# P.V in the step of its own scores, exp in four masked pieces, and a reordered last projection in a cached-attention decode kernel

## The chip, the cores and the metric

The kernel runs on one core of a Trainium2 chip. Times are device microseconds (us) of one launch. A profiled execution also gives a trace; its span (first to last instruction) is some 2 us under the launch time. Engines are PE (matrix products; PEld is its weight load), DVE (vector), ACT (activation functions), POOL, and SP, whose queue issues nearly all loads. "Rate" is what the DMA engines moved, in GB/s. The granted clock is the share of PE's full clock that the trace shows as granted.

All comparisons use runs in the fast state; a run counts as slow when it is over 1.5% above the fastest of its kernel. A ratio is the mean time of one kernel's fast runs over that of the other's fast runs of the same rounds, so it is not quite the ratio of the medians that are quoted.

## The reference

One decode step for four sequences, in bf16: attention over a cache, then an MLP, each behind a layernorm, with residuals.

```python
q = layernorm(x) @ wq                        # x [4,1,640], wq [640, 32*128]
scores = einsum("bhqd,bhkd->bhqk", q, k_cache) * 128 ** -0.5   # k_cache [4,32,4096,128]
o = einsum("bhqk,bhkd->bhqd", softmax(scores), v_cache)        # v_cache as k_cache
h = x + o.reshape(4, 1, 4096) @ wo           # wo [4096, 640]
hm = layernorm(h) @ w1 + b1                  # w1 [640, 1728]
out = h + (hm * tanh(softplus(hm))) @ w2     # w2 [1728, 640]
```

The two caches are 134 MB each; they are nearly all of the 283 MB that the kernel reads, and each byte is used once.

## The kernel before

The work is cut into 32 tiles, one for each group of four heads and each sequence. A tile is 4 MB of K and 4 MB of V. Partition p holds 128 keys of head p // 32. All K and V tiles go through a pool of four slots of 32 KB per partition; a load waits until a slot is free.

```python
NSLOT = 4; G = 4; PG = 32; R = 128; RS = 32; NSUB = 4; NE = 3
...
loads = []                                  # order: k0 v0 k1 v1 ... k29 v29 k30 k31 v30 v31 wo w1 w2
...
def issue_loads(upto):                      # called as issue_loads(i + 1) at the start of step i
    while loads and not (upto < NT and upto in kt and upto in vt):
        f, *a = loads.pop(0)
        f(*a)
```

A tile is handled in four parts s. DVE multiplies K by q, PE folds the products of 128 columns to 16 by adding them in PSUM (the memory that takes its sums), DVE sums these to scores. After the fourth part ACT takes exp four times, once for each head: head g sits in 32 partitions, and its exp is written to column g of a buffer that was cleared once, so that P.V gets a block-diagonal left side.

```python
def emit_scores(i, s):
    ...
    nc.vector.tensor_reduce(out=s_t[i][:, s * RS : (s + 1) * RS], in_=reds.pop((i, s))[:, :, :], ...)
    if s == NSUB - 1:
        for g in range(G):
            sl = slice(g * PG, (g + 1) * PG)
            nc.scalar.activation(out=e_bufs[i % NE][sl, :, g], in_=s_t[i][sl, :], func=ACT.Exp,
                scale=SCALE, accum_out=rs_bufs[hg % 2][sl, b, g : g + 1])
...
for i in range(NT):
    issue_loads(i + LA)
    for s in range(NSUB):
        emit_mult(i, s)
        if s > 0:
            emit_scores(i, s - 1)
        elif i > 0:
            emit_scores(i - 1, NSUB - 1)     # last part of the tile before
            ...
        emit_fold(i, s)
        if i > 0 and i < last:
            emit_pv(i - 1, s)                # P.V of the tile before
        ...
```

After the loop come P.V of the last tiles and the last projection. For each group k, `emit_wo(k)` permutes the attention output on PE, copies it to bf16 on DVE and multiplies it by `wo`.

```python
emit_pv(last, 2); emit_pv(last, 3); emit_pv_copy(last)
for k in range(WLATE, NWB - 1):             # groups 4, 5, 6
    emit_wo(k)
emit_o(last); emit_ot(NHG - 1); emit_wo(NWB - 1)
```

The softmax here doesn't subtract the row's maximum and nothing guards it: scores larger than these inputs give would overflow.

## Time and profile before

| | before |
|---|---|
| time, median of the first 3 runs | 686.46 us (682.96 to 686.54) |
| span of the profiled run | 682.5 us |
| busy: PE, DVE, ACT | 65%, 56%, 14% |
| moved over DMA | 283.8 MB |

The page of the profile, its share line and its DMA lines. In the DMA line each digit is the busy share of one fortieth of the span, in tenths; the next line has the GB/s of the same slices.

```profile
PE 444.8 (65%) x2933; PEld 179.6 (26%) x2933; DVE 380.9 (56%) x329; ACT 96.2 (14%) x311; POOL 3.6 (1%) x14
...
DMA  9999999999999999999999999999999999999991
GB/s 366 438 427 432 418 438 431 429 404 436 429 427 419 431 432 429 434 425 416 442 428 436 414 432 433 427 421 427 432 434 422 414 430 430 430 397 425 415 412 69
```

No engine but the DMA is near its limit. The DMA is busy to the end of the 39th slice. The rate is not flat. Between the second slice and the 39th it goes from 397 to 442 while the busy digit stays at 9.

Now one step of the loop, from the timeline (start, duration, engine and line, what it does; in brackets the idle time before and what ended it):

```profile
206.22 2.29 DVE L284 TENSOR_TENSOR prod<-k_1049,qbc 128x4096 bf16<-128x4096 bf16 x1 [3.04 <-DMA k_1049<-in_A_k_cache_dram]
...
219.56 2.28 DVE L284 TENSOR_TENSOR prod<-k_1049,qbc 128x4096 bf16<-128x4096 bf16 x1
...
221.87 0.33 SPq L95 DMA_DIRECT2D v_1150<-in_A_v_cache_dram  x1
...
225.25 0.33 SPq L95 DMA_DIRECT2D k_1304<-in_A_k_cache_dram  x1
...
226.30 2.29 DVE L284 TENSOR_TENSOR prod<-k_1148,qbc 128x4096 bf16<-128x4096 bf16 x1 [3.27 <-DMA k_1148<-in_A_k_cache_dram]
```

The tile `k_1049` is worked from 206.2. The V of the next tile, `v_1150`, is issued only when the last multiply of this one ends (221.84), because the other three slots are still held: by the V of the tile before (its P.V runs in this step), by this tile's V and by the next K. At that moment the only other load under way is `k_1148`, which lands 4.4 us later; by issues less bytes moved, 1.0 MB was left to move.

The stretch from 10 to 640 us, from the view by windows (busy time of PE, PEld, DVE, ACT and POOL, then granted PE clock, DMA share, GB/s):

```profile
10.00:640.00 630.00, 413.21 (x2513) 158.58 (x2513) 361.18 (x268) 86.77 (x289) 0.00 (x0) 0.82 1.00 427
```

And the tail on PE, with one copy on DVE, from the timeline:

```profile
652.27 0.60 PE L320 MATMUL l_ps<-rs_136,ones_f 128*128 128x16 f32 x2 [2.90 <-ACT e_130 L313]
...
652.81 3.59 PE L332 MATMUL pv_122<-v_3298,e_128 128*16 128x512 bf16 x32
...
656.18 1.92 PE L332 MATMUL pv_124<-v_3392,e_130 128*16 128x512 bf16 x16
...
659.33 1.04 PE L332 MATMUL pv_124<-v_3392,e_130 128*16 128x512 bf16 x16
...
664.32 1.85 PE L353 MATMUL o_ps<-selo,pv_sb 128*128 128x4 f32 x8
...
668.00 0.18 DVE L440 COPY st<-y_ps 128x20 f32<-128x20 f32 x1 [0.77 <-PE y_ps L385]
...
670.80 4.72 PE L497 MATMUL h_ps<-ln_3821,w_slot 128*64 128x4 bf16 x70 [1.60 <-DVE ln_3821 L477]
```

PE waits 2.9 us for the last tile's exp, then does P.V of the last two tiles, then the projections one after another; from the last P.V group to the copy of the projection's sum (`y_ps`) it is 8.7 us. The MLP's first product starts at 670.8.

### The profile page before, as it was taken

To read this page: it belongs to the slowest core of one execution; us is meant where nothing else is said; L and a number is where in the kernel's file an instruction comes from. 1 tells how busy PE (TensorE), PEld (TensorE's weight loads), DVE (VectorE), ACT (ScalarE), POOL (GpSimd) and SP (SyncE) were. 2 spreads that over 40 slices of the span, in tenths; PEclk is the share of its full clock that TensorE was granted. 3 is DMA by queue.
4 is the path that set the end of the run, shared out by engine and by line. 5 is a ranking of instruction groups with operands and counts; after the bars stand their busy time and mean duration, and the time that the engine had idled before them with its cause. 6 is when DMAs were issued, how large, how long until landed. Compare 5 with 4: busy or idle time off the path is not lost.

```text
span 682.5 us, 6833 instructions
## 1 busy us (share of the span) xinstructions
PE 444.8 (65%) x2933; PEld 179.6 (26%) x2933; DVE 380.9 (56%) x329; ACT 96.2 (14%) x311; POOL 3.6 (1%) x14
## 2 busy tenths in 40 slices
PE   1836674773676844786647756767547777475876
PEld 0312221231223312232212322223112222121445
DVE  3445565583566744756645755666546556547902
ACT  0301111110111111011111101111111011111121
POOL 2000000000000000000000000000000000000000
PEclk9968976887877867989768888688788887678975
DMA  9999999999999999999999999999999999999991
GB/s 366 438 427 432 418 438 431 429 404 436 429 427 419 431 432 429 434 425 416 442 428 436 414 432 433 427 421 427 432 434 422 414 430 430 430 397 425 415 412 69
DMA packets 13014, 283.80 MB, mean 416 GB/s; under 512 B 1652, under 2 KB 1720, under 8 KB 3768
## 3 DMA queue, kind: packets, MB, share of 16 engines
q1 hardware_dynamic: 12656, 283.27, 97.4%
q8 instruction: 23, 0.38, 0.2%
q10 hardware_dynamic: 328, 0.09, 0.1%
q14 instruction: 7, 0.06, 0.0%
HBM read 283.35 MB, written 0.01 MB: 415 GB/s over the span
## 4 chain that ended last, share of the span: by engine, by line
DMA 53%; PE 33%; DVE 8%; ACT 3%; issue 2%; DVEq 0%; ACTq 0%
PE red L296 20%; DVE prod L284 6%; PE pv_124 L332 5%; DMA k_1846<-in_A_k_cache_dram 4%; DMA k_1400<-in_A_k_cache_dram 4%; DMA k_3100<-in_A_k_cache_dram 4%; DMA k_412<-in_A_k_cache_dram 4%; DMA k_2290<-in_A_k_cache_dram 4%; DMA k_2695<-in_A_k_cache_dram 4%; DMA k_603<-in_A_k_cache_dram 3%; DMA k_2040<-in_A_k_cache_dram 3%; DMA k_3294<-in_A_k_cache_dram 3%; DMA k_858<-in_A_k_cache_dram 3%; DMA k_2484<-in_A_k_cache_dram 3%; DMA k_1594<-in_A_k_cache_dram 3%; DMA k_1148<-in_A_k_cache_dram 3%
## 5 line engine op out<-in xcount | busy, mean ns | idle before, releaser
L296 PE MATMUL red<-prod,ident 128*128 128x512 bf16 x1024 | 297.2, 443 | 142.1 <-DVE prod L284 141.8
L296 PEld LDWEIGHTS <-ident 128*128 128x128 bf16 x1024 | 107.2, 111 | 310.2 <-issue 242.3
L305 DVE TENSOR_REDUCE s_f<-red 128x32 f32<-128x512 f32 x128 | 87.9, 687 | 34.3 <-PE red L296 33.9
L353 PEld LDWEIGHTS o_ps<-selo,pv_sb 128*128 128x128 f32 x256 | 32.2, 197 | 13.5 <-issue 10.3
L343 ACT COPY pv_sb<-pv_122 128x512 f32<-128x512 f32 x16 | 9.4, 586 | 183.0 <-PE pv_122 L332 183.0
L353 PE MATMUL o_ps<-selo,pv_sb 128*128 128x4 f32 x256 | 34.8, 259 | 0.0
L343 ACT COPY pv_sb<-pv_124 128x512 f32<-128x512 f32 x16 | 9.4, 586 | 171.4 <-PE pv_124 L332 171.4
L313 ACT ACTIVATE e_130<-s_f 32x128 bf16<-32x128 f32 x44 | 21.3, 485 | 61.4 <-DVE s_f L305 60.8
L313 ACT ACTIVATE e_128<-s_f 32x128 bf16<-32x128 f32 x44 | 21.3, 484 | 52.8 <-DVE s_f L305 52.3
L313 ACT ACTIVATE e_132<-s_f 32x128 bf16<-32x128 f32 x40 | 19.4, 484 | 54.0 <-DVE s_f L305 53.6
L320 PE MATMUL l_ps<-rs_134,ones_f 128*128 128x16 f32 x8 | 2.4, 381 | 37.6 <-ACT e_128 L313 19.2
L320 PE MATMUL l_ps<-rs_136,ones_f 128*128 128x16 f32 x8 | 2.4, 381 | 31.6 <-ACT e_132 L313 9.7
L284 DVE TENSOR_TENSOR prod<-k_82,qbc 128x4096 bf16<-128x4096 bf16 x4 | 9.1, 2284 | 17.7 <-DMA k_82<-in_A_k_cache_dram 17.7
L359 DVE TENSOR_TENSOR OT<-o_ps,rl 128x16 bf16<-128x16 f32 x8 | 1.6, 195 | 28.1 <-PE o_ps L353 28.1
L284 DVE TENSOR_TENSOR prod<-k_858,qbc 128x4096 bf16<-128x4096 bf16 x4 | 9.1, 2284 | 10.3 <-DMA k_858<-in_A_k_cache_dram 10.3
L284 DVE TENSOR_TENSOR prod<-k_1750,qbc 128x4096 bf16<-128x4096 bf16 x4 | 9.1, 2284 | 9.7 <-DMA k_1750<-in_A_k_cache_dram 9.7
L284 DVE TENSOR_TENSOR prod<-k_248,qbc 128x4096 bf16<-128x4096 bf16 x4 | 9.1, 2284 | 9.4 <-DMA k_248<-in_A_k_cache_dram 9.4
L284 DVE TENSOR_TENSOR prod<-k_412,qbc 128x4096 bf16<-128x4096 bf16 x4 | 9.1, 2285 | 9.4 <-DMA k_412<-in_A_k_cache_dram 9.4
L284 DVE TENSOR_TENSOR prod<-k_1304,qbc 128x4096 bf16<-128x4096 bf16 x4 | 9.1, 2284 | 9.3 <-DMA k_1304<-in_A_k_cache_dram 9.3
L326 DVE RECIPROCAL rl<-l_ps 128x16 f32<-128x16 f32 x8 | 2.1, 258 | 21.9 <-PE l_ps L320 21.9
L256 PE MATMUL q_ps<-wq_74,lnT 128*4 128x512 bf16 x32 | 11.1, 470 | 3.9 <-DMA wq_74<-in_A_wq_dram 3.9
L284 DVE TENSOR_TENSOR prod<-k_2194,qbc 128x4096 bf16<-128x4096 bf16 x4 | 9.1, 2284 | 8.0 <-DMA k_2194<-in_A_k_cache_dram 8.0
(159 smaller groups left out, 460.4 us busy)
## 6 DMA issues: line engine op xcount, KB each, us to landing
wq_74<-in_A_wq_dram SPq DMA_DIRECT2D x4, 1024.0 KB, 9.7
k_82<-in_A_k_cache_dram SPq DMA_DIRECT2D x1, 4096.0 KB, 20.5
v_84<-in_A_v_cache_dram SPq DMA_DIRECT2D x1, 4096.0 KB
k_248<-in_A_k_cache_dram SPq DMA_DIRECT2D x1, 4096.0 KB
v_250<-in_A_v_cache_dram SPq DMA_DIRECT2D x1, 4096.0 KB
k_300<-in_A_k_cache_dram SPq DMA_DIRECT2D x1, 4096.0 KB
v_302<-in_A_v_cache_dram SPq DMA_DIRECT2D x1, 4096.0 KB, 16.8
k_412<-in_A_k_cache_dram SPq DMA_DIRECT2D x1, 4096.0 KB
```

The source lines that it names most:

```text
L256: nc.tensor.matmul(q_ps[:, :], lhsT=lnT[:, c, :], rhs=wq_t[c // WQC][:, o : o + 512], start=(c == 0), stop=(c == DC - 1),)
L284: nc.vector.tensor_tensor(out=t[:, :, :], in0=kt[i][:, s * RS : (s + 1) * RS, :], in1=q_bc[hg][:, b, :].unsqueeze(1).to_broadcast([P, RS, ...
L296: nc.tensor.matmul(red[:, :, :], lhsT=ident[:, :], rhs=t[:, :, c * CW : (c + 1) * CW], start=(c == 0), stop=(c == Dh // CW - 1),)
L305: nc.vector.tensor_reduce(out=s_t[i][:, s * RS : (s + 1) * RS], in_=reds.pop((i, s))[:, :, :], axis=AX.X, op=ALU.add,)
L313: nc.scalar.activation(out=e_bufs[i % NE][sl, :, g], in_=s_t[i][sl, :], func=ACT.Exp, scale=SCALE, accum_out=rs_bufs[hg % 2][sl, b, g : g ...
L320: nc.tensor.matmul(l_ps[hg][:, :], lhsT=ones_f[:, :], rhs=rs_bufs[hg % 2][:, :, :].rearrange("p b g -> p (b g)"), start=True, stop=True,)
L326: nc.vector.reciprocal(out=rl[hg][:, :], in_=l_ps.pop(hg)[:, :])
L332: nc.tensor.matmul(pvs[i % 2][k * QD : k * QD + RQ * G, :], lhsT=e_bufs[i % NE][:, u * RQ : (u + 1) * RQ, :], rhs=vt[i][:, u * RQ : (u + 1 ...
L343: nc.scalar.copy(out=pv_sb[i][:, :, :].rearrange("p r d -> p (r d)"), in_=pvs[i % 2][:, :])
L353: nc.tensor.matmul(o_ps[hg][:, b, :], lhsT=t[:, r, :], rhs=selo[:, r, :], start=(r == 0), stop=(r == RQ - 1),)
L359: nc.vector.tensor_tensor(out=OT[:, hg * G : (hg + 1) * G, :].rearrange("p g b -> p b g"), in0=o_ps.pop(hg)[:, :, :], in1=rl.pop(hg)[:, :] ...
```

## The change

It aims at freeing V slots a step earlier, at a shorter chain after the last scores, and at a shorter tail. P.V of tile i moves from step i+1 to the end of step i. Exp is taken after each quarter of a tile on all 128 partitions, and a 0/1 mask on DVE spreads it over the four head columns. In the tail, permutations of earlier groups are done in their own steps, and the weight products are ordered to fill waits. The list of loads is rewritten but gives the same order.

```diff
+        nc.scalar.activation(                      # emit_scores, every s
+            out=ex_t[i][:, sl], in_=s_t[i][:, sl], func=ACT.Exp,
+            scale=SCALE, accum_out=rs_t[hg][:, b, s : s + 1],
+        )
+    def emit_mask(i, s):
+        nc.vector.tensor_tensor(
+            out=e_t[i][:, sl, :],
+            in0=ex_t[i][:, sl].unsqueeze(2).to_broadcast([P, RS, G]),
+            in1=hmask[:, :].unsqueeze(1).to_broadcast([P, RS, G]), op=ALU.mult)
 ... (the three cleared e buffers and two rs buffers go; the sums are masked too)
             if s > 0:
                 emit_scores(i, s - 1)
-            elif i > 0:
-                emit_scores(i - 1, NSUB - 1)
-            ...
+            if s > 1:
+                emit_mask(i, s - 2)
             emit_fold(i, s)
-            if i > 0 and i < last:
-                emit_pv(i - 1, s)
+            ... emit_o(i - 1), emit_ot, emit_perm, emit_wo of the group before at s = 1, 2, 3
+        emit_scores(i, NSUB - 1)
+        emit_mask(i, NSUB - 2)
+        emit_mask(i, NSUB - 1)
+        if i < last - 1:
+            for s in range(NSUB):
+                emit_pv(i, s)
+            emit_pv_copy(i)
 ... (tail)
-    for k in range(WLATE, NWB - 1):
-        emit_wo(k)
     emit_o(last)
     emit_ot(NHG - 1)
-    emit_wo(NWB - 1)
+    emit_wo(WLATE)
+    emit_wo(WLATE + 1)
+    emit_perm(NHG - 1)
+    emit_wo(WLATE + 2)
+    emit_wo(WLATE + 3)
 ... (layernorm: the square moves from DVE to ACT, 1/D into the matrix of ones)
```

More of the change, by code (lines that the diff above doesn't have):

```diff
@@ L137 @@
         loads.append((load_cache, kt, A_k_cache, i, "k"))
-        if i < NT - 2:
-            loads.append((load_cache, vt, A_v_cache, i, "v"))
-    loads.append((load_cache, kt, A_k_cache, NT - 1, "k"))
-    loads.append((load_cache, vt, A_v_cache, NT - 2, "v"))
+        if i == NT - 2:
+            loads.append((load_cache, kt, A_k_cache, NT - 1, "k"))
+        loads.append((load_cache, vt, A_v_cache, i, "v"))
     loads.append((load_cache, vt, A_v_cache, NT - 1, "v", 4))
@@ L196 @@
     )
-    for k in range(NE):
-        e = consts.tile([P, R, G], BF16, name=f"e{k}")
-        nc.gpsimd.memset(e[:, :, :], 0.0)
-        e_bufs.append(e)
-    rs_bufs = []
-    for k in range(2):
-        r = consts.tile([P, N, G], FP32, name=f"rs{k}")
-        nc.gpsimd.memset(r[:, :, :], 0.0)
-        rs_bufs.append(r)
+    hmask_f = consts.tile([P, G], FP32)
+    hmask = consts.tile([P, G], BF16)
+    nc.vector.tensor_reduce(
+        out=hmask_f[:, :], in_=ident[:, :].rearrange("p (g q) -> p g q", g=G), axis=AX.X, op=ALU.add
+    )
+    nc.vector.tensor_copy(out=hmask[:, :], in_=hmask_f[:, :])
+    ones_d = consts.tile([P, P], FP32)
+    nc.vector.memset(ones_d[:, :], 1.0 / D)
     IW = D // CG
@@ L300, in emit_fold @@
         reds[i, s] = red
+    e_t, ex_t, rs_t = {}, {}, {}
     def emit_scores(i, s):
+        hg, b = tiles[i]
         if s == 0:
             s_t[i] = work.tile([P, R], FP32, tag="s_f", name="s_f")
+            ex_t[i] = work.tile([P, R], BF16, tag="ex", name="ex")
+            e_t[i] = work.tile([P, R, G], BF16, tag="e", name="e", bufs=NE)
+            if b == 0:
+                rs_t[hg] = work.tile([P, N, NSUB], FP32, tag="rs", name="rs")
+        sl = slice(s * RS, (s + 1) * RS)
         nc.vector.tensor_reduce(
-            out=s_t[i][:, s * RS : (s + 1) * RS], in_=reds.pop((i, s))[:, :, :],
-            axis=AX.X, op=ALU.add,
-        )
-        if s == NSUB - 1:
-            hg, b = tiles[i]
-            for g in range(G):
-                sl = slice(g * PG, (g + 1) * PG)
-                nc.scalar.activation(
-                    out=e_bufs[i % NE][sl, :, g], in_=s_t[i][sl, :], func=ACT.Exp,
-                    scale=SCALE, accum_out=rs_bufs[hg % 2][sl, b, g : g + 1],
-                )
-    def emit_sum(hg):
+            out=s_t[i][:, sl], in_=reds.pop((i, s))[:, :, :], axis=AX.X, op=ALU.add
+        )
+        nc.scalar.activation(
+            out=ex_t[i][:, sl], in_=s_t[i][:, sl], func=ACT.Exp,
+            scale=SCALE, accum_out=rs_t[hg][:, b, s : s + 1],
+        )
+    def emit_mask(i, s):
+        sl = slice(s * RS, (s + 1) * RS)
+        nc.vector.tensor_tensor(
+            out=e_t[i][:, sl, :],
+            in0=ex_t[i][:, sl].unsqueeze(2).to_broadcast([P, RS, G]),
+            in1=hmask[:, :].unsqueeze(1).to_broadcast([P, RS, G]),
+            op=ALU.mult,
+        )
+    def emit_sum(hg):
+        rs1 = work.tile([P, N], FP32, tag="rs1", name="rs1")
+        nc.vector.tensor_reduce(
+            out=rs1[:, :], in_=rs_t.pop(hg)[:, :, :], axis=AX.X, op=ALU.add
+        )
+        rsm = work.tile([P, N, G], FP32, tag="rsm", name="rsm")
+        nc.vector.tensor_tensor(
+            out=rsm[:, :, :], in0=rs1[:, :].unsqueeze(2).to_broadcast([P, N, G]),
+            in1=hmask[:, :].unsqueeze(1).to_broadcast([P, N, G]), op=ALU.mult,
+        )
         l_ps[hg] = ps.tile([P, N * G], FP32, tag="misc", name="l_ps")
@@ L321, in emit_sum @@
             l_ps[hg][:, :], lhsT=ones_f[:, :],
-            rhs=rs_bufs[hg % 2][:, :, :].rearrange("p b g -> p (b g)"),
-            start=True, stop=True,
+            rhs=rsm[:, :, :].rearrange("p b g -> p (b g)"), start=True, stop=True,
         )
@@ L333, in emit_pv @@
                 pvs[i % 2][k * QD : k * QD + RQ * G, :],
-                lhsT=e_bufs[i % NE][:, u * RQ : (u + 1) * RQ, :],
+                lhsT=e_t[i][:, u * RQ : (u + 1) * RQ, :],
                 rhs=vt[i][:, u * RQ : (u + 1) * RQ, :],
@@ L369, with emit_perm @@
     )
-    def emit_wo(k):
+    a_t = {}
+    def emit_perm(k):
         a_ps = ps.tile([P, WB, N], FP32, tag="misc", name="a_ps")
@@ L379, in emit_wo @@
                 )
-        a = work.tile([P, WB, N], BF16, tag="a", name="a_bf")
-        nc.vector.tensor_copy(out=a[:, :, :], in_=a_ps[:, :, :])
+        a_t[k] = consts.tile([P, WB, N], BF16, name=f"a{k}")
+        nc.vector.tensor_copy(out=a_t[k][:, :, :], in_=a_ps[:, :, :])
+    def emit_wo(k):
         t = wo_t.pop(k)
@@ L385, in emit_wo @@
                 nc.tensor.matmul(
-                    y_ps[:, c, :], lhsT=t[:, j, c * P : (c + 1) * P], rhs=a[:, j, :],
+                    y_ps[:, c, :], lhsT=t[:, j, c * P : (c + 1) * P], rhs=a_t[k][:, j, :],
                     start=False, stop=(k == NWB - 1 and j == WB - 1 and c == DC - 1),
@@ L403 @@
                 emit_scores(i, s - 1)
-            elif i > 0:
-                emit_scores(i - 1, NSUB - 1)
-                if b == 0:
-                    emit_sum(hg - 1)
-            emit_fold(i, s)
-            if i > 0 and i < last:
-                emit_pv(i - 1, s)
-            if i > 1 and s == 1:
-                emit_o(i - 2)
-                if b == 1:
-                    emit_ot(hg - 1)
-                    if hg <= WLATE:
-                        emit_wo(hg - 1)
-        if i == last:
-            emit_scores(i, NSUB - 1)
+            if s > 1:
+                emit_mask(i, s - 2)
+            emit_fold(i, s)
+            if i > 0 and s == 1 and i < last:
+                emit_o(i - 1)
+                if b == 0:
+                    emit_ot(hg - 1)
+            if b == 0 and i > 0 and s == 2:
+                emit_perm(hg - 1)
+            if b == 0 and i > 0 and s == 3 and hg <= WLATE:
+                emit_wo(hg - 1)
+        emit_scores(i, NSUB - 1)
[5 more added lines that the diff above has]
+            emit_pv_copy(i)
+        if b == N - 1:
             emit_sum(hg)
-            for s in range(NSUB):
-                emit_pv(i - 1, s)
-        if i > 0:
-            emit_pv_copy(i - 1)
         if b == 1 and hg + 1 < NHG:
             emit_qbc(hg + 1)
+    for s in range(NSUB):
+        emit_pv(last - 1, s)
+    emit_pv_copy(last - 1)
     emit_pv(last, 0)
@@ L431 @@
     emit_pv_copy(last)
-    for k in range(WLATE, NWB - 1):
-        emit_wo(k)
     emit_o(last)
     emit_ot(NHG - 1)
-    emit_wo(NWB - 1)
+    emit_wo(WLATE)
[3 more added lines that the diff above has]
+    emit_wo(WLATE + 3)
     st = consts.tile([P, 2, DC, N], FP32)
     nc.vector.tensor_copy(out=st[:, 0, :, :], in_=y_ps[:, :, :])
-    nc.vector.tensor_tensor(
-        out=st[:, 1, :, :], in0=st[:, 0, :, :], in1=st[:, 0, :, :], op=ALU.mult
-    )
+    nc.scalar.activation(out=st[:, 1, :, :], in_=y_ps[:, :, :], func=ACT.Square)
     s_ps = ps.tile([P, 2 * DC * N], FP32, tag="misc", name="s_ps")
     nc.tensor.matmul(
-        s_ps[:, :], lhsT=ones_f[:, :], rhs=st[:, :, :, :].rearrange("p k c n -> p (k c n)"),
+        s_ps[:, :], lhsT=ones_d[:, :], rhs=st[:, :, :, :].rearrange("p k c n -> p (k c n)"),
         start=True, stop=True,
@@ L460 @@
     )
-    nc.vector.tensor_scalar_mul(out=mu[:, :, :], in0=mu[:, :, :], scalar1=1.0 / D)
     msq = consts.tile([P, N], FP32)
```

## The prediction

> **What bounds it now.** The load stream. The page's slice table has the DMA engines at nine tenths or more in 39 of 40 slices; in one-microsecond windows all but a last fraction of the 283.8 MB has moved by 668 us of 682.5 (about 426 GB/s from 3 us on). The Trainium skill (DMA: Bandwidth & Descriptors, Specifications) gives a fabric ceiling of 435 GB/s, so about 2% of rate is left; the best stretches here hold 431 to 438. PE is busy 65%, DVE 56%, ACT 14%. In the timeline DVE waits 2.5 to 10 us for each K tile. A serial tail follows: y_ps complete at 667.97, layernorm to 670.8, first MLP product 4.7, mish 1.7, second product 2.2, store: 14.5 us without loads.
>
> **What the change does.**
> 1. Loads. Their order is unchanged; slots come free earlier. Before, P.V of tile i-1 runs in step i, so three slots are held when loads of tile i+1 are wanted: in the timeline its v is issued only after the last multiply of tile i (221.9 us; its K lands at 226.3), the K after that when P.V ends (225.3). Bytes issued but not moved fall under 1 MB in many steps. After, both slots of tile i-1 are free at the end of step i-1, so k and v of i+1 go out one tile (4.2 MB, about 9.8 us) earlier; I estimate that 7 MB stay outstanding. In ten- and twenty-microsecond windows the trace moves 418 to 422 GB/s where outstanding bytes fell below 1 MB, 431 where they did not (overall 427). All at 431, the stream ends 6 us earlier; I count on 4.
> 2. Tail. Permutations of groups 4 to 6 (each 0.55, a 0.17 cast, 0.6 of waits) leave the tail; wo(4), wo(5) fill the wait for OT, wo(6) that for the last cast. From the last P.V product (660.3) to y_ps I count 5.2 us for 7.7: 2.5 saved. Square on ACT beside the copy, and 1/D folded into the ones matrix, save 0.3. I expect no further ACT table load.
> 3. Cost. Four masks per tile on DVE, estimated 0.25 us each from the small DVE operations here; exp in four 128x32 pieces is no dearer than four 32x128 ones of 0.485+0.25. P.V waits for its last mask, and DVE has no multiply ahead of the last reduction: about 3 us bubble per step. I estimate a step of 17 to 18 us against 19.5 of loads, so it hides. At the end it costs perhaps 1 us.
>
> **Sum.** About 4 + 2.8 - 1 = 6 us, 0.9%. Predicted 680.3 us, range 674 to 686. Chance of faster by over 2%: 0.09; within 2%: 0.87; slower by over 2%: 0.04.
>
> **What would show each step.** (1) V issues no longer follow the multiplies of the tile before by a few us; the DMA rate over 10 to 640 us rises from 427 to 430 or more; DVE still waits several us for K. (2) From last P.V product to the y_ps copy about 5 us; one group of perm matmuls there. (3) Mask operations near 0.25 us; every step ends before the next K lands.
>
> **What would make it wrong.** If rate dips are the memory's own, only the tail's 2 us remain. If a step at the slow PE clock (0.5 granted in stretches) exceeds 19.5 us, the kernel becomes compute bound and slower. If the stream ends earlier but the last tile's chain does not follow, less is gained.

## The result

| | before | after |
|---|---|---|
| median, first comparison (4 runs each) | 685.25 us (682.96 to 686.54) | 675.52 us (674.76 to 677.62) |
| ratio of fast runs | | 0.9867 (95%: 0.9828 to 0.9905) |
| two more comparisons, medians of fast runs (11 runs before each) | 683.29, 684.00 | 677.03, 676.90; ratios 0.9912, 0.9896 |
| span of the profiled run | 682.5 | 673.0 |

So the change wins 0.9% to 1.3%, 6 to 9 us. The same lines after, first the page:

```profile
PE 431.2 (64%) x2933; PEld 192.9 (29%) x2933; DVE 410.7 (61%) x474; ACT 75.4 (11%) x312; POOL 1.9 (0%) x9
...
DMA  9999999999999999999999999999999999999993
GB/s 368 425 428 434 442 427 422 432 434 439 428 424 432 433 437 428 425 429 435 433 430 428 429 429 435 428 432 433 432 429 430 431 429 433 430 430 433 414 415 160
```

DVE has become busier and the kernel faster: DVE did not bound it. The rate line is flatter; between the second and the 37th slice nothing is under 422. The windows:

```profile
10.00:640.00 630.00, 406.91 (x2574) 176.68 (x2574) 392.95 (x410) 68.10 (x295) 0.00 (x0) 0.84 1.00 431
```

427 has become 431. One step of the loop, from the timeline:

```profile
203.85 0.33 SPq L95 DMA_DIRECT2D k_1292<-in_A_k_cache_dram  x1
...
208.77 4.49 DVE L283 TENSOR_TENSOR prod<-k_1150,qbc 128x4096 bf16<-128x4096 bf16 x2
...
209.80 0.33 SPq L95 DMA_DIRECT2D v_1294<-in_A_v_cache_dram  x1
...
224.96 2.29 DVE L283 TENSOR_TENSOR prod<-k_1292,qbc 128x4096 bf16<-128x4096 bf16 x1 [2.55 <-DMA k_1292<-in_A_k_cache_dram]
```

K and V of a tile now both go out at the end of the step two before their own, K after the last multiply and V after P.V: `k_1292` at 203.85 and `v_1294` at 209.80, and `k_1292` is waited for until 224.96, 21 us after its issue. That time is not what changed: before, `k_1148` went out at 205.40 and was waited for until 226.30, 21 us as well. What changed is how much was still to be moved at the moments when a slot came free: 1.0 MB when `v_1150` went out before, 3.7 MB when `k_1292` goes out after. The tail:

```profile
649.35 0.39 PE L340 MATMUL l_ps<-rsm,ones_f 128*128 128x16 f32 x2 [1.75 <-DVE rsm L335]
...
649.68 1.90 PE L351 MATMUL pv_122<-v_3605,e 128*16 128x512 bf16 x32
...
651.41 1.04 PE L351 MATMUL pv_124<-v_3705,e 128*16 128x512 bf16 x16
...
653.36 1.04 PE L351 MATMUL pv_124<-v_3705,e 128*16 128x512 bf16 x16
...
655.14 1.06 PE L372 MATMUL o_ps<-selo,pv_sb 128*128 128x4 f32 x8 [0.74 <-ACT pv_sb L362]
...
658.68 0.18 DVE L468 COPY st<-y_ps 128x20 f32<-128x20 f32 x1 [0.87 <-PE y_ps L408]
...
661.22 4.74 PE L522 MATMUL h_ps<-ln_4048,w_slot 128*64 128x4 bf16 x70 [1.39 <-DVE ln_4048 L502]
```

Where the 9.5 us of span between these two traces come from, step by step (starts; the 31st K tile is the last one that DVE waits for):

| | before | after | gained by then |
|---|---|---|---|
| first multiply of the 31st K tile | 623.72 | 619.31 | 4.4 |
| first P.V of the last two tiles | 652.81 | 649.68 | 3.1 |
| last P.V group | 659.33 | 653.36 | 6.0 |
| copy of `y_ps` | 668.00 | 658.68 | 9.3 |
| first MLP product | 670.80 | 661.22 | 9.6 |

The stream gains 4.4 us, the chain of the last two tiles gives 1.3 back, the P.V products themselves gain 2.8 and the new tail 3.3. The P.V part needs care: in the stretch from 652 to 658 us the trace before has a granted clock of 0.5 and the trace after 1.0. The experiments show which of these are the change's.

To look at the first part, I worked out how much was under way at each moment: bytes issued (issue times in the timeline, with the size of each load) minus bytes moved (windows of one microsecond). Before, from 60 to 600 us, the least is 0.1 MB and the mean 5.1 MB; after, 3.4 MB and 9.0 MB. Sorting windows of ten microseconds (one starts at each microsecond, so they overlap) before 600 us by the least that was outstanding in them:

| | under 1 MB | 1 to 3 MB | 3 MB and more |
|---|---|---|---|
| before: mean rate (windows) | 420 (116) | 431 (207) | 429 (257) |
| after: mean rate (windows) | none | 432 (11) | 431 (569) |

The 431 GB/s of after is about the rate that before had whenever more than 1 MB was outstanding. The edges of the classes are soft: a recount from the packed trace puts the first cell at 415 to 420, by where within an issue its bytes are counted.

### The profile page after: what moved, and what is told of

Same layout as the page of the kernel before. It is cut to its first block, busy times and chain, and to the rows that moved or that the text cites. A ratio compares the mean times of both kernels' runs of the same rounds, so it can differ in the third digit from the quotient of the medians.

```text
span 673.0 us, 6966 instructions
## 1 busy us (share of the span) xinstructions
PE 431.2 (64%) x2933; PEld 192.9 (29%) x2933; DVE 410.7 (61%) x474; ACT 75.4 (11%) x312; POOL 1.9 (0%) x9
## 4 chain that ended last, share of the span: by engine, by line
DMA 59%; DVE 19%; PE 19%; issue 1%; ACT 0%; SPq 0%; DVEq 0%; ACTq 0%
DVE prod L283 16%; PE red L295 14%; DMA k_342<-in_A_k_cache_dram 4%; DMA k_1516<-in_A_k_cache_dram 4%; DMA k_1041<-in_A_k_cache_dram 4%; DMA k_1991<-in_A_k_cache_dram 4%; DMA k_566<-in_A_k_cache_dram 4%; DMA k_2464<-in_A_k_cache_dram 4%; DMA k_3370<-in_A_k_cache_dram 4%; DMA k_2917<-in_A_k_cache_dram 4%; DMA k_3148<-in_A_k_cache_dram 4%; DMA k_1767<-in_A_k_cache_dram 4%; DMA k_817<-in_A_k_cache_dram 3%; DMA k_2695<-in_A_k_cache_dram 3%; DMA k_3601<-in_A_k_cache_dram 3%; DMA k_1292<-in_A_k_cache_dram 3%
## 5 line engine op out<-in xcount | busy, mean ns | idle before, releaser
L295 PE MATMUL red<-prod,ident 128*128 128x512 bf16 x1024 | 302.3, 454 | 218.7 <-DVE prod L283 217.7
L295 PEld LDWEIGHTS <-ident 128*128 128x128 bf16 x1024 | 116.5, 115 | 386.1 <-issue 319.7
L315 ACT ACTIVATE ex<-s_f 128x32 bf16<-128x32 f32 x128 | 29.4, 229 | 518.0 <-DVE s_f L312 518.0
L322 DVE TENSOR_TENSOR e<-ex,hmask 128x128 bf16<-128x128 bf16 x128 | 36.4, 284 | 6.1 <-ACT ex L315 6.1
L351 PEld LDWEIGHTS <-e 128*16 128x16 bf16 x1024 | 18.4, 88 | 45.8 <-DVE e L322 21.8
L372 PE MATMUL o_ps<-selo,pv_sb 128*128 128x4 f32 x256 | 30.6, 243 | 0.7 <-ACT pv_sb L362 0.7
L315 ACT ACTIVATION_READ_ACCUMULATOR ex<-s_f 128x1 f32 x128 | 23.8, 186 | 0.0
L283 DVE TENSOR_TENSOR prod<-k_82,qbc 128x4096 bf16<-128x4096 bf16 x4 | 9.1, 2286 | 17.9 <-DMA k_82<-in_A_k_cache_dram 17.9
L283 DVE TENSOR_TENSOR prod<-k_244,qbc 128x4096 bf16<-128x4096 bf16 x4 | 9.1, 2286 | 6.7 <-DMA k_244<-in_A_k_cache_dram 6.7
L283 DVE TENSOR_TENSOR prod<-k_1415,qbc 128x4096 bf16<-128x4096 bf16 x4 | 9.1, 2285 | 6.7 <-DMA k_1415<-in_A_k_cache_dram 6.7
L283 DVE TENSOR_TENSOR prod<-k_3148,qbc 128x4096 bf16<-128x4096 bf16 x4 | 9.1, 2285 | 6.3 <-DMA k_3148<-in_A_k_cache_dram 6.3
L283 DVE TENSOR_TENSOR prod<-k_940,qbc 128x4096 bf16<-128x4096 bf16 x4 | 9.1, 2287 | 6.1 <-DMA k_940<-in_A_k_cache_dram 6.1
L283 DVE TENSOR_TENSOR prod<-k_1767,qbc 128x4096 bf16<-128x4096 bf16 x4 | 9.1, 2285 | 5.9 <-DMA k_1767<-in_A_k_cache_dram 5.9
L283 DVE TENSOR_TENSOR prod<-k_1890,qbc 128x4096 bf16<-128x4096 bf16 x4 | 9.1, 2287 | 5.7 <-DMA k_1890<-in_A_k_cache_dram 5.7
L283 DVE TENSOR_TENSOR prod<-k_465,qbc 128x4096 bf16<-128x4096 bf16 x4 | 9.1, 2286 | 5.7 <-DMA k_465<-in_A_k_cache_dram 5.7
L283 DVE TENSOR_TENSOR prod<-k_2363,qbc 128x4096 bf16<-128x4096 bf16 x4 | 9.1, 2285 | 5.6 <-DMA k_2363<-in_A_k_cache_dram 5.6
L283 DVE TENSOR_TENSOR prod<-k_2695,qbc 128x4096 bf16<-128x4096 bf16 x4 | 9.1, 2286 | 5.1 <-DMA k_2695<-in_A_k_cache_dram 5.1
L283 DVE TENSOR_TENSOR prod<-k_3601,qbc 128x4096 bf16<-128x4096 bf16 x4 | 9.1, 2284 | 5.1 <-DMA k_3601<-in_A_k_cache_dram 5.1
```

The source lines that it names most:

```text
L283: nc.vector.tensor_tensor(out=t[:, :, :], in0=kt[i][:, s * RS : (s + 1) * RS, :], in1=q_bc[hg][:, b, :].unsqueeze(1).to_broadcast([P, RS, ...
L295: nc.tensor.matmul(red[:, :, :], lhsT=ident[:, :], rhs=t[:, :, c * CW : (c + 1) * CW], start=(c == 0), stop=(c == Dh // CW - 1),)
L315: nc.scalar.activation(out=ex_t[i][:, sl], in_=s_t[i][:, sl], func=ACT.Exp, scale=SCALE, accum_out=rs_t[hg][:, b, s : s + 1],)
L322: nc.vector.tensor_tensor(out=e_t[i][:, sl, :], in0=ex_t[i][:, sl].unsqueeze(2).to_broadcast([P, RS, G]), in1=hmask[:, :].unsqueeze(1).to_ ...
L351: nc.tensor.matmul(pvs[i % 2][k * QD : k * QD + RQ * G, :], lhsT=e_t[i][:, u * RQ : (u + 1) * RQ, :], rhs=vt[i][:, u * RQ : (u + 1) * RQ, ...
L372: nc.tensor.matmul(o_ps[hg][:, b, :], lhsT=t[:, r, :], rhs=selo[:, r, :], start=(r == 0), stop=(r == RQ - 1),)
```

## The experiments

Theory "depth": most of the gain is that one load more (4.2 MB) is always queued, so that the 16 DMA engines no longer run short at the end of a load. The rest is work taken from the tail. Rivals: the rate rose through something else (the masks, the exp, chance); the tail gained only through the PE clock; or DVE or PE bound the loop.

Times of one chip, before on the same chip 682.7 us (mean of 12): the first eight runs below. All results were correct.

### The changed kernel again

No edit; a reference for the runs beside it.

> The changed kernel once more, as the reference for the runs beside it. Both theories: 674 to 678 us, ratio to before about 0.986; DMA rate between 10 and 640 us 430 to 431 GB/s against 427 before; last P.V products at granted clock 1.0 and y_ps copied near 658.7 us of a span of 673.

Mean of the five fast runs 676.62 us, ratio 0.9912 (0.9875 to 0.9950). Its first execution, the profiled one, took 1306 us and counts for nothing here: 1024 fold products at a mean of 1088 ns, against 454 in the first trace. Why that one execution had slow products is not known. The profile was taken anew in a later run (`after_third`).

### Three slots: the loads as late as before

```diff
-    NSLOT = 4
+    NSLOT = 3        # V of tile 0 and K of tile 31 have a buffer of their own
 ... (in load_cache: the tag that gives them that buffer)
```

With P.V in its own step but one slot fewer, V of tile i+1 again waits for the last multiply of tile i, and the K after it for P.V. At the end of the kernel the loads are as in the changed kernel.

> The changed kernel with three tile slots in place of four for all but the first V and the last K tile, so that loads go out as late as they did before, everything else of the change kept. Theory depth (the rate dips before came from too few bytes outstanding): the rate over 10 to 640 us falls back to about 427 GB/s, the 31st K tile lands 4 us later than in the changed kernel (623 for 619), time 4 to 5 us above it (about 680). Rival (the rate rose because of something else in the change, or by chance): rate stays 430 to 431 and the time within 1.5 us of the changed kernel.

Mean 684.60 us, ratio to before 1.0029 (0.9992 to 1.0066): 8.0 us slower than the changed kernel, and the whole gain is gone. The windows of its trace:

```profile
10.00:640.00 630.00, 409.40 (x2556) 176.81 (x2556) 385.32 (x402) 67.44 (x291) 0.00 (x0) 0.83 0.99 424
```

The rate is under that of before, and the 31st K tile comes at 629.0. A step shows why:

```profile
241.60 0.33 SPq L99 DMA_DIRECT2D v<-in_A_v_cache_dram  x1
...
245.64 0.33 SPq L99 DMA_DIRECT2D k<-in_A_k_cache_dram  x1
...
250.69 2.29 DVE L287 TENSOR_TENSOR prod<-k,qbc 128x4096 bf16<-128x4096 bf16 x1 [5.76 <-DMA k<-in_A_k_cache_dram]
```

Loads follow the multiplies again. In ten-microsecond windows with under 1 MB outstanding the rate is 378 GB/s (74 windows); in all others it is 430 to 433 up to 6 MB; so it is not that the tiles lie elsewhere in this run. Depth is shown, and more strongly than I had expected: the rest of the change lengthens a step (DVE no longer has a multiply ahead of the last reduction), so without the extra slot it drains the queue deeper than the kernel before did. The two other parts of the change, worth some 2 us in the tail, cannot make up for that.

### Only the move of P.V

The changed kernel with the old exp (no masks) and the old tail.

```diff
         # emit_scores, s == NSUB - 1: the old four exps, head by head, into cleared buffers
+                nc.scalar.activation(out=e_t[i][gl, :, g], in_=s_t[i][gl, :], func=ACT.Exp, ...)
     def emit_mask(i, s):
+        return
 ... (the five cleared buffers are back, the sums need no mask; the old tail as in the next run)
```

> Only the move of P.V into the step of its own scores (with what it does to the slots): exp is again four 32-partition pieces at the end of a tile without masks, the tail is the old one. Theory depth: rate 430 to 431 as in the changed kernel, so about 4 us faster than before at the 31st K tile; but the last tile's exp is now bare, 2.9 us in place of about 0.9, so the end gives some 2 us back (more if PE falls to half clock in the wait): 681 to 684, 1 to 4 us below before. Rival (masks and exp pieces are what matter): no faster than before and rate 427.

Mean 677.68 us, ratio 0.9921 (0.9881 to 0.9960): 5.0 us faster than before (2.7 to 8.1 by the interval), by one part of the change alone, where 1 to 4 us were expected. The 31st K tile starts at 617.35, 6.4 us earlier than before, and the rate from 10 to 600 us is 433:

```profile
10.00:600.00 590.00, 387.40 (x2406) 172.08 (x2404) 337.76 (x251) 83.20 (x277) 0.00 (x0) 0.86 1.00 433
```

The rival is out: masks and exp pieces are not what raised the rate. The profiled execution is the slowest of the six (680.12): in it the last P.V ran at half clock, as in the first trace of before.

```profile
648.13 0.61 PE L342 MATMUL l_ps<-rs,ones_f 128*128 128x16 f32 x2 [2.90 <-ACT e L324]
...
648.66 5.30 PE L353 MATMUL pv<-v,e 128*16 128x512 bf16 x48
```

### The changed kernel with the old tail

```diff
-    emit_o(last)
-    emit_ot(NHG - 1)
-    emit_wo(WLATE)
-    ...
+    for k in range(WLATE, NWB - 1):
+        emit_perm(k)
+        emit_wo(k)
+    emit_o(last)
+    emit_ot(NHG - 1)
+    emit_perm(NHG - 1)
+    emit_wo(NWB - 1)
 ... (groups 4 to 6 are no longer permuted in their own steps; the old layernorm lines)
```

> The changed kernel with the old last projection (permutation of groups 4 to 7 after the last P.V, old order) and the old layernorm lines. Theory tail by work moved: 2.5 to 3.3 us slower than the changed kernel (678 to 679). Rival (the tail won 3.5 us only because the PE clock was higher there): under 1.5 us slower. Rate unchanged at 430 to 431.

Mean 678.99 us, 2.4 us slower than the changed kernel on the same chip, with the rate at 431. The tail is worth 2.4 us by the work moved, just under the 2.5 to 3.3 that were reckoned. In its trace the last P.V ran at full clock too, so the PE clock does not explain the difference there. But the mean is also 1.3 us above that of only moving P.V, though its exp chain is shorter. The six runs of that kernel spread over 4 us, so the times alone don't show this difference; but the rates of the two traces differ (431 and 433), and the last runs below take that up.

### The kernel before with the new tail

The same tail edit, the other way round, in the kernel before.

> The kernel before with only the new tail: permutations of groups 4 to 6 done in their own steps, the last projection in the new order, Square on ACT and 1/D folded in. Tail by work moved: 2.5 to 3.3 us faster than before, rate 427 as before. Rival (tail gain was PE clock): under 1.5 us faster.

Mean 680.40 us, ratio 0.9970 (0.9922 to 1.0018): 2.3 us faster at the middle, but the interval holds none too, so it is unclear by itself. It agrees in size with the run above. Its trace shows a limit that the tail meets here:

```profile
661.33 0.68 PE L391 MATMUL y_ps<-a,wo_late 128*128 128x4 bf16 x20 [0.22 <-DMA wo_late<-in_A_wo_dram]
662.92 0.69 PE L391 MATMUL y_ps<-a,wo_late 128*128 128x4 bf16 x20 [0.92 <-DMA wo_late<-in_A_wo_dram]
```

With the slower stream, the last weights have not landed when the tail wants them. In this trace PE also ran the last P.V at full clock (32 and 16 products in 2.77 us) after the same wait, without any edit to that end:

```profile
652.86 0.39 PE L322 MATMUL l_ps<-rs,ones_f 128*128 128x16 f32 x2 [2.90 <-ACT e L315]
653.18 2.77 PE L334 MATMUL pv<-v,e 128*16 128x512 bf16 x48
```

### The kernel before with PE kept busy

```diff
         if i == last:
+            for c in range(13):      # result unused
+                nc.tensor.matmul(warm, lhsT=ident[:, :], rhs=vt[last - 1][:, 0:RQ, :], ...)
             emit_scores(i, NSUB - 1)
```

> The kernel before with 13 idle 512-column matmuls (result unused) put on PE after the last fold, where it waited 2.9 us for the exp of the last tile. Theory clock: the last two tiles' P.V run at granted clock 1.0 in place of 0.5, about 4.7 us from first to last product in place of 7.5, so 2 to 3 us faster than before. Rival (the products' time there was set by data or waits): no change, within 1 us.

Mean 682.27 us, ratio 0.9995 (0.9960 to 1.0030). In its trace the granted clock from 640 to 660 us is 1.00 (0.83 before), and the chain from the first multiply of the 31st K tile to the start of the last projection's last group is 40.7 us (624.86 to 665.56) for 43.6 (623.72 to 667.29), 2.9 us shorter as reckoned. In the times none of it is seen; the interval allows at most 2.7 us. How often an execution has the half clock there is not known. Of the five traces with this wait of 2.9 us, two had it for all of the first 48 products (before, and only P.V moved: 5.30 us), one for a part (`ko_oldexp`, 4.45 us) and two not at all (the run above and `a_oldexp`, 2.77 us). Of the seven with the wait of 1.75 us that the new exp leaves, six had full clock and one (three slots, 4.35 us) had it in part. So the half clock belongs to no one kernel, and how much of the 2.8 us in the step-by-step table the change saves on average stays open. They are not counted for it here.

### Masks three times

```diff
+        for _ in range(3 if i < last - 1 else 1):
             nc.vector.tensor_tensor(out=e_t[i][:, sl, :], ... op=ALU.mult)
```

> The changed kernel with every mask done three times, but for the last two tiles: 8 more DVE operations of 0.28 us, 2.3 us more DVE work in every step. Theory loads bound the loop: steps of 15 us grow to 17 or so, under the 19.5 us of loads, and the time stays within 1 us of the changed kernel. Rival (DVE is on the path in the loop): up to 2.3 times 30 = 68 us slower.

Mean 675.52 us, 1.1 us under the changed kernel, so no slower, with DVE busy 459.5 us for 392.9 from 10 to 640 us and the rate at 431:

```profile
10.00:640.00 630.00, 412.60 (x2571) 176.46 (x2571) 459.54 (x649) 68.11 (x295) 0.00 (x0) 0.85 1.00 431
```

DVE has that much room in the loop. No run loads PE; but in the changed kernel DVE waits 2 to 7 us for a K load before all tiles from the second to the 31st except those that follow the first tile of a head group (from the second group on), so PE did not bound the loop as a whole.

### The last K tiles one load earlier

After the 31st K tile the changed kernel has 53.7 us of serial work left (619.3 to 673.0), more than the loads that follow. So bring those K tiles forward.

```diff
-    order: k29 v29 k30 k31 v30 v31         (in words, not the lines of the edit)
+    order: k29 k30 v29 k31 v30 v31         # P.V of tile 29 runs in step 30
```

> The changed kernel with the last K tiles one load earlier (order k29 k30 v29 k31 v30 v31) and P.V of tile 29 deferred into step 30. Theory: after the 31st K tile has landed the end is a serial DVE and PE chain of 53 us against 45 us of loads, so the chain is what bounds the end; with that K 9.8 us earlier DVE's 5 us wait before it goes and y_ps comes 4 to 5 us earlier: 671 to 672 us. Rival (the end is bound by the loads of the last V and the weights): within 1.5 us of the changed kernel.

Mean 672.39 us (671.90 to 672.84), ratio to before 0.9850 (0.9817 to 0.9884): 4.2 us faster than the changed kernel on the same chip, and faster than both kernels. The first multiply of each of the last two tiles, from the timeline:

```profile
617.28 4.49 DVE L287 TENSOR_TENSOR prod<-k,qbc 128x4096 bf16<-128x4096 bf16 x2
...
632.42 4.49 DVE L287 TENSOR_TENSOR prod<-k,qbc 128x4096 bf16<-128x4096 bf16 x2
```

No wait stands before them any more (5.1 us for the 31st K tile in the changed kernel), and the last tile starts at 632.42 for 634.42. The two traces differ by only 2.0 us there and 2.5 us in span: the first trace of the changed kernel is of its fastest execution (674.76), while the 4.2 us are between means on one chip. The last group of the projection now waits 0.25 us for the `wo` weights: chain and loads end nearly together.

### What the masks and pieces cost

Three runs on another chip (before there: 684.3, mean of 11), for the 1.3 us left open above.

> The changed kernel again beside the two runs below, since its profile failed last time and since masks and exp are now to be weighed to a few tenths of a per cent: 675 to 677 us, rate over 10 to 600 us 431 GB/s.

Mean 676.62 us, ratio 0.9896 (0.9849 to 0.9944), rate 431.

> The changed kernel with the old exp (four 32-partition pieces at the end of a tile, no masks, old sums), new tail kept. The run of only the P.V move came out 1.9 us under the one with masks and exp pieces added, against my reckoning that the new exp shortens the end by about 1 us. Theory cost (masks and exp pieces cost time): 673.5 to 675, 1.5 to 2 us under the changed kernel, and a rate of 432 to 433. Theory saving (the earlier difference was chance): 676 to 678, equal or 1 us above the changed kernel, rate 431.

The edit is the old exp as in the run that only moves P.V, the tail new. Mean of the five fast runs 674.60 us, 2.0 us under the changed kernel. Its profiled execution was slow, with 387 to 414 GB/s over its first 200 us, so its time is not used.

> The kernel with the last K tiles one load earlier, with the old exp. Theory cost: 670 to 671.5, under the 672.4 of its like with masks. Theory saving: 672 to 674.

Mean 672.17 us, ratio 0.9824 (0.9779 to 0.9868), as fast as its like with masks (672.39, other chip), so this one doesn't tell the theories apart by time. Its rate does: 432.3.

So the versions with the old exp have the faster stream. Three masks in place of one did not slow it, so it is not the masks' traffic. What else differs is that the old exp needs five cleared buffers of its own, so that other buffers can come to lie elsewhere in memory. The last run puts these back, unused:

```diff
+    for k in range(NE):
+        e = consts.tile([P, R, G], BF16, name=f"e{k}")     # cleared, never read
+        nc.gpsimd.memset(e[:, :, :], 0.0)
+    ... (two of [P, N, G] FP32 likewise)
     hmask_f = consts.tile([P, G], FP32)
```

> The changed kernel with the old exp's cleared buffers (three of 1 KB, two of 64 B per partition) put back unused, so that the tile slots lie where they lie with the old exp while exp and masks stay new. Three masks in place of one left the rate at 431, so the mask's traffic is not what makes the rate 431 here against 432 to 433 with the old exp. Theory place: rate over 10 to 600 us 432 to 433 and some 2 us under the changed kernel (about 674.5). Theory exp (the new exp's instructions or their timing): rate 431, time as the changed kernel (675.5 to 677).

Mean 673.94 us (a third chip; before there 682.9), ratio 0.9871 (0.9838 to 0.9904). The rate, from five-microsecond windows over 10 to 600 us:

| without the five buffers | GB/s | with the five buffers | GB/s |
|---|---|---|---|
| changed kernel, first trace and `after_third` | 431.0, 431.0 | only P.V moved | 432.6 |
| old tail | 431.0 | old exp, early K | 432.3 |
| three masks | 430.9 | buffers put back, new exp | 432.6 |
| early K | 431.2 | | |

The two columns do not overlap, and the last run has the new exp and the masks in the fast column. The start of the 31st K tile agrees: 617.35 and 617.77 (only P.V moved, buffers put back) against 619.31 to 620.17 in the first four traces of the left column. At 283 MB, 431.0 against 432.6 is 2.4 us. This points to the presence of the five buffers, not to the exp, and the masks cost nothing that these runs see. It is not as firm as the depth: the last run is one trace on a chip where the changed kernel did not run, and its ratio (0.9871) is not apart from those of the changed kernel (0.9867, 0.9912, 0.9896). As the buffers are never read, where they leave the others to lie is the likeliest cause; that is an argument by exclusion, no run shows the addresses, and what about the place would matter stays open. The kernel before has the buffers too, and its undrained stretches moved 429 to 431, so having them is not enough by itself.

## Why the prediction was right or wrong

It was right in direction, class and range: 680.3 with 674 to 686 was forecast, and the medians of the fast runs were 675.5, 677.0 and 676.9. The gain was 6 us in the forecast and 6 to 9 us in the three comparisons. Part of that closeness is luck: the stream gained more than the 4 us of the forecast where the five buffers stayed (6.4 us at the 31st K tile with only P.V moved), and in the changed kernel some 2 us that nobody foresaw took it back to 4.4.

- "What bounds it now": right. The stream bounds the loop; DVE could take 17% more work (459.5 for 392.9 us) at no cost in time.
- Step 1, loads: the mechanism was right. With the old depth the gain is gone (684.6); with only the move of P.V most of it is there (677.7 for 682.7). The size, "I count on 4", fits the 5.0 that the move alone measured (2.7 to 8.1), and the rate rose all the way to that of undrained stretches. The fear that the dips might be "the memory's own" fell. "I estimate that 7 MB stay outstanding" was too high for a floor: the least was 3.4 MB, the mean 9.0.
- Step 2, tail: 2.8 us forecast, 2.4 measured by undoing it. In the traces the time from the last P.V group to `y_ps` went from 8.7 to 5.3 us; it was 8.4 in the run with the old tail, which had full clock in P.V, so little of it is clock. As forecast, no further table load: both traces have two of 1.28 us in the tail.
- Step 3, cost: masks measure 284 ns (0.25 forecast), the chain of the last two tiles lengthened by 1.3 us (1 forecast). "Every step ends before the next K lands" failed, and with it the estimate of "17 to 18 us against 19.5 of loads": in the changed kernel the step of the first tile of a head group (from the second group on), with the permutation in it, took 20.2 us in five of seven cases and 22.7 and 23.1 us in the two where the granted clock was lowest (0.70 and 0.71; one runs from 186.05 to 208.77), and the next tile starts without a wait. The others take some 14 to 17 us. The rate did not fall for it (431 from 186 to 209 us), as loads were queued; the forecast had looked at one step for all.
- Not foreseen: with the five cleared buffers gone, the stream takes some 2 us longer (by the rates; the cause is argued, not shown). It hid in the changed kernel as if it were the price of the masks.

The Trainium skill (DMA: Bandwidth & Descriptors, Specifications) puts the fabric ceiling at 435 GB/s; 431 to 433 over 590 us stays just under it, so by that figure hardly anything is left there. On the PE clock the skill (TensorE: Matmul & The Clock Gate, HAM oscillation) has the rule of thumb of no idle gap above about 3.4 us; the first trace of before and that of only moving P.V fell to half clock in a gap of 2.9 us, and the trace of before with the new tail stayed at full clock after a gap of the same 2.9 us. A single trace is thus a poor witness for a tail of this kind.

## What to carry to other kernels

A DMA share of 1.00 does not mean that the stream runs at full rate: work out the bytes outstanding over time, and if they come near zero, look at which consumer holds a buffer longest and move it, before adding anything else. Once the stream is full, the end of the kernel is a race between the last loads and the serial chain behind the last tile that is waited for; ordering the loads for that chain was worth another 4.2 us here. And when an edit adds or drops buffers, check with an unused stand-in whether part of what it did comes from that alone.

## What the Trainium skill lacked or had wrong

- DMA: Bandwidth & Descriptors has sizes per transfer (425 GB/s at 16 MB) but not how much must be queued behind a running load. Here with 4 MB loads the rate held 429 to 433 with 1 MB or more outstanding, and fell to 420 (before) and 378 (three slots) in ten-microsecond windows where it went below 1 MB.
- No page that I read gives a number for what a shift of the buffers in SBUF by a few KB does to the rate of a stream of large loads. Here it was 431.0 GB/s without and 432.6 with 3.1 KB per partition of unused buffers; whether the place of the others is the cause, and why, is open.
- ScalarE: Activation LUTs, What ACT_TABLE_LOAD costs: its 1283 ns per load agrees (1.28 us in the traces). Its 2.66 us for a whole switch is not seen: in the changed kernel the square ends at 659.08, the load starts at 659.10, and the square root starts at 660.45, 1.37 us in all.
- TensorE: Matmul & The Clock Gate, HAM oscillation: the gap of about 3.4 us is not a safe limit; two traces fell to 0.5 in a wait of 2.9 us, and two with the same wait did not. And products of four columns hardly notice the clock: 20 of them took 0.64 us at clock 1.0 and 0.68 at 0.5.
